# Fused convolution and gated feed-forward: the opening's mask, first convolution and the place of w_out's second half

## The chip, the cores and the metric

The kernel runs on one core of one Trainium2 chip. The metric is the device time of one execution in microseconds (us). A core has five engines with queues of their own: TensorE (PE in the profile, its weight loads PEld), VectorE (DVE), ScalarE (ACT), GpSimd (POOL) and SyncE (SP). Transfers are asked for from a queue (SPq, POOLq, ACTq) and then run in the core's DMA rings.

## The reference

Eight heads share a causal convolution of 7 taps along the sequence, its taps normalized by softmax; the result goes through a feed-forward with the gate h * cos(h).

```python
w = softmax(weight, axis=-1)                       # (8 heads, 7 taps)
out[b, s, h, :] = sum_k w[h, k] * x_pad[b, s + k, h, :]   # x: (8, 4096, 192), 24 columns a head
t = out.reshape(32768, 192)
h = t @ w_in                                       # w_in: (192, 2048)
result = (h * cos(h)) @ w_out                      # w_out: (2048, 192), float32
```

## The kernel before, in words

**Units and tiles.** The 32768 tokens are worked in 32 units of 1024 tokens (u) and 64 tiles of 512 (t); a block is 128 tokens. For each unit x is loaded in float32 (`load_unit`, L75; the rows at block edges by `load_edges`, L69), cast to bfloat16 on GpSimd (`cast_unit`, L185), convolved on TensorE by a banded matrix that holds the taps (`conv_part`, L196), evicted from PSUM (L209, L211), doubled (`double_unit`, L260) and transposed by a DMA (`turn_unit`, L269); the edges are mended on GpSimd (`mend_edges`, L288 to L300). Each tile then runs eight first matmuls h0 to h7 (`mm1`, L398; 12 or 6 matmuls of 512 columns), cosine on ScalarE and the product on VectorE (`gcu`, L405, L409), and the second matmul in 64 steps (`mm2_step`, L442), evicted and stored (L453, L456).

**Order.** Nothing is reordered by a scheduler: the program's order is the order on each engine (`manual_schedule`). `PE_ORDER`/`PE_FIRST` and `ACT_ORDER`/`ACT_FIRST` write out by hand, for each tile, the order on TensorE (h0.. first matmuls, m5 five steps of the second, c1, c2, d1, d2, r convolutions, p and q the ends of the second matmul's halves) and on ScalarE. At half of the second matmul two matmuls that share a bank are ordered by `Turn`: a no-operation in SyncE's queue (L169) waits for the one, and the other waits for it. So TensorE can stand still for whatever is ahead of that instruction in SyncE's queue, and DMAs are issued from the same queue, in order.

**Opening.** Before the loop the following is prepared:

- Four blocks of unit 0 are loaded first (SyncE, L75). GpSimd makes `quarter` (L112 to L115), then asks for w_in in two loads of 384 KB (L85), which it casts to bfloat16 on the way.
- `keep_warm` (L108) runs matmuls on zeros. One small matmul (L124) spreads the taps over partitions; softmax follows on VectorE and ScalarE (L147 to L158).
- `shifted` (L131, L132) is a diagonal of ones, 134 wide; its last 128 columns are the identity for transposes. Four copies of 32x44 of it (`rows32`, L142, L153), read with overlapping rows by the hand-made access pattern `mask`, times the taps give `prod` (L308), whose sum is `diag` (L311). When that is done SyncE goes on to the other loads of units 0 and 1. Sixteen copies spread `diag` to the banded matrix `band` (L322), on VectorE, GpSimd and ScalarE.
- `conv_first` (L340) convolves unit 0's first four blocks in four PSUM banks, quarter of the heads by quarter; four evictions (L346). After the last, SyncE loads w_out in four loads of 384 KB (L96): `load_wo(0)` the first half, `load_wo(1)` the second.
- `turn_first` (L361, L364) transposes these blocks on TensorE, since the first matmuls need them soon.
- Unit 0's other four blocks go through `conv_rest` in tile 0 (r, L196, evicted at L209) and a DMA transpose (L269), which is followed in SyncE's queue by the loads of units 2 and 3 (L75, L69) and, in tile 1, by the transpose of unit 1.
- w_out is cast on GpSimd in two halves (`cast_wo`, L92): the first in tile 0, the second after `double_unit(1)`.

Of the kernel before, what the change touches and what calls it, by code (L numbers as in the profile page):

```python
# [8 lines left out]
FP32 = mybir.dt.float32  # L9
BF16 = mybir.dt.bfloat16  # L10
AF = mybir.ActivationFunctionType
ALU = mybir.AluOpType
# [4 lines left out]
def kernel(  # L17
# [8 lines left out]
    nc = tc.nc  # L26
# [57 lines left out]
    def load_w(t):  # L84
        nc.gpsimd.dma_start(out=w[64 * t : 64 * t + 64].rearrange("p k j f -> p k (j f)"), in_=w_src[t])  # L85
# [8 lines left out]
    def load_wo(q):  # L94
        for i in range(2):
            nc.sync.dma_start(out=wo_f[:, q * HP : (q + 1) * HP, i], in_=wo_src[:, q * HP : (q + 1) * HP, i])  # L96
# [9 lines left out]
    def keep_warm(n, bank=idle):  # L106
        for _ in range(n):
            nc.tensor.matmul(out=bank, lhsT=zero[:, 0:128], rhs=zero, start=True, stop=True)  # L108
# [5 lines left out]
                            channel_multiplier=-32)  # L114
    nc.gpsimd.affine_select(out=quarter, in_=quarter, compare_op=ALU.is_ge, fill=0.0, base=31, pattern=[[-1, 128]],  # L115
                            channel_multiplier=32)
    for t in range(2):
        load_w(t)
    scrap = consts.tile([128, 1], FP32)
    nc.scalar.activation(out=scrap, in_=one, func=AF.Exp)  # L120
    keep_warm(3)
# [5 lines left out]

    xb0 = xbf_pool.tile([128, UB + 1, D], BF16, name="x_bf")

    shifted = consts.tile([128, 128 + K - 1], BF16)  # L130
    nc.gpsimd.memset(shifted, 0.0)  # L131
    nc.gpsimd.affine_select(out=shifted, in_=shifted, compare_op=ALU.not_equal, fill=1.0, base=1 - K,  # L132
                            pattern=[[1, 128 + K - 1]], channel_multiplier=-1)
    ident = shifted[:, K - 1 :]
    band = consts.tile([128, H, 256], BF16)
    nc.vector.memset(band, 0.0)

    E = 32 + K - 1
    rows32 = consts.tile([128, E + K - 1], BF16)
    mask = bass.AP(rows32.tensor, rows32.offset, [rows32.ap[0], [0, HQ], [1, E], [1, K]])  # L140
    for q in (1, 2):
        nc.gpsimd.tensor_copy(out=rows32[32 * q : 32 * q + 32], in_=shifted[0:32, 0 : E + K - 1])  # L142
    nc.gpsimd.memset(xb0[:, 0, :], 0.0)
    wn = consts.tile([128, HQ, K], BF16)

    wmax = consts.tile([128, HQ, 1], FP32)
# [2 lines left out]
    nc.vector.tensor_tensor(out=wexp, in0=w_bc, in1=wmax.to_broadcast([128, HQ, K]), op=ALU.subtract)  # L149
    nc.scalar.activation(out=wexp, in_=wexp, func=AF.Exp)  # L150
    nc.scalar.activation(out=scrap, in_=one, func=AF.Sin)
    for q in (0, 3):
        nc.vector.tensor_copy(out=rows32[32 * q : 32 * q + 32], in_=shifted[0:32, 0 : E + K - 1])  # L153
    wsum = consts.tile([128, HQ, 1], FP32)
    nc.vector.tensor_reduce(out=wsum[:, :, 0], in_=wexp, axis=mybir.AxisListType.X, op=ALU.add)
    winv = consts.tile([128, HQ, 1], FP32)
# [56 lines left out]
    def ring_banks():  # L213
        h = h_pool.tile([128, 2, T], FP32, name="h")
        return [h[:, 0, :], h[:, 1, :]]

    def o_banks():
        return [o_pools[b].tile([128, T], FP32, name="o_ps%d" % b) for b in range(2)]
# [46 lines left out]
    def turn_unit(u, n0=0, n1=UB + 1):  # L265
        ct = ct_tiles.pop(u)
        if u not in cT:
            cT[u] = cT_pool.tile([128, UB + 1, NC, 128], BF16, name="cT")
        nc.sync.dma_start_transpose(out=cT[u][:, n0:n1].rearrange("p n c k -> p (n c) k"),  # L269
                                    in_=ct[:, n0:n1].rearrange("p n c t k -> p (n c t k)"))  # L270
        cT.pop(u - 2, None)
# [13 lines left out]
    def mend_edges(u):  # L285
# [12 lines left out]
        for j in (1, 2):  # L298
# [6 lines left out]
    cast_unit(0, 0, NB, nc.scalar.copy)  # L305

    prod = consts.tile([128, HQ, E, K], BF16)
    nc.vector.tensor_tensor(out=prod, in0=mask,  # L308
                            in1=wn.rearrange("p h (o k) -> p h o k", o=1).to_broadcast([128, HQ, E, K]), op=ALU.mult)
    diag = consts.tile([128, HQ, E], FP32)  # L310
    summed = nc.vector.tensor_reduce(out=diag, in_=prod, axis=mybir.AxisListType.X, op=ALU.add)  # L311
# [20 lines left out]

    def conv_first():

        banks = o_banks() + ring_banks()
        for q in range(4):
            for n in range(NB):
                for h in range(HQ * q, HQ * (q + 1)):
                    for prev in range(2):
                        nc.tensor.matmul(  # L340
                            out=banks[n][:, 0:D].rearrange("p (k h r) -> p h k r", k=NC, h=H)[:, h],
                            lhsT=band[:, h, 128 * prev : 128 * prev + 128],
                            rhs=bf[0][:, n + 1 - prev, h * G : (h + 1) * G].rearrange("p (k r) -> p k r", k=NC),
                            start=(h == 0 and prev == 0), stop=(h == H - 1 and prev == 1), skip_group_check=True)
        for n in range(NB):
            m = copies[n % 2](out=ct_tiles[0][:, n],  # L346
                              in_=banks[n][:, 0:D].rearrange("p (m t w) -> p m t w", t=1, w=64).to_broadcast([128, NC, 2, 64]))
        tc.add_manual_dep(nc.sync.nop().ins, m.ins.name, sync_dep, reason="order of the transfers")
        load_wo(0)
        load_wo(1)  # L350

    def turn_first(half):
        banks = o_banks() if half else None
        for n in range(2):
            ps = banks[n] if half else ring_banks()
            if not half:
                if n == 0:
                    keep_warm(1, ps[1])
                ps = ps[0]
            for k in range(NC):  # L360
                nc.tensor.matmul(out=ps[:, k * 128 : (k + 1) * 128],  # L361
                                 lhsT=ct_tiles[0][:, 2 * half + n, k, :, :].rearrange("p t w -> p (t w)"), rhs=ident,
                                 start=True, stop=True, skip_group_check=True)
            copies[n](out=cT[0][:, 2 * half + n].rearrange("p c k -> p (c k)"), in_=ps[:, 0 : NC * 128])  # L364
# [118 lines left out]
    for t in range(NT + 2):  # L483
        u, second = divmod(t, TPU)
        cu, cc = (u + TPU, second) if t >= TPU else (1 + t, 1)
        conv = {"c": conv_part(cu, cc, ring_banks if t else o_banks, t < TPU) if cu < NU else iter(())}
        if t < TPU:
            conv["d"] = conv_part(cu, 0, ring_banks if t else o_banks, True)
        if t == 0:
            conv["r"] = conv_rest()  # L490
        act, done, h = (ACT_ORDER if t >= len(ACT_FIRST) else ACT_FIRST[t]).split(), set(), {}

        def flush():
            while act:
                k = act[0]
                need = {"P": "p", "Q": "p", "e": "r" if k == "er" else k[1:2] + "2"}.get(k[0], "h" + k[1:])
                if need not in done:
                    return
                act.pop(0)
                if k[0] in "PQ":  # L500
                    if 0 <= t - 2 < NT - 1:
                        evac(t - 2, "PQ".index(k[0]))
                elif k[0] == "e":
                    next(conv[k[1]], None)
                    if k == "er":
                        turn_unit(0, NB, UB)
                        load_unit(2)
                        load_edges(2)
                        cast_wo(0)
                elif k[0] == "s" and t < NT:  # L510
                    gcu(t, int(k[1]), h.pop(k[1:]), *HALVES[k[2:]])

        for k in (PE_ORDER if t >= len(PE_FIRST) else PE_FIRST[t]).split():
            if k[0] == "h" and t < NT:
                h[k[1:]] = mm1(t, int(k[1]), *HALVES[k[2:]])
            elif k[0] in conv:
                next(conv[k[0]], None)
            elif k[0] == "m":
                for q in range(step, step + int(k[1:])):
                    mm2_step(q)  # L520
                step += int(k[1:])
            elif k[0] == "p":
                assert step % (2 * STEPS) == 0
            elif k[0] == "q":
                assert step % (2 * STEPS) == STEPS
            done.add(k)
            flush()

            if k == "q":
                if second == 0 and t and u + 1 < NU:  # L530
                    mend_edges(u + 1)
                if t == 1:
                    cast_unit(3)
                    mend_edges(1)
                if second == 0 and u + 3 < NU:
                    cast_unit(u + 3)
            if k == "p":
                if second == 1 and t > 1 and cu < NU:
                    double_unit(cu)
                if second == 0 and t and u + 1 < NU:  # L540
                    turn_unit(u + 1)
                if t == 1:
                    turn_unit(1)
                if 0 <= t - 2 < NT - 1:
                    store(t - 2)
                if t == NT + 1:
                    finish(NT - 1)
            if k == ("p" if t > 1 else "q") and second == 1 and u + 4 < NU:
                load_unit(u + 4)
                load_edges(u + 4)  # L550
        if t == 0:
            double_unit(1)
            cast_wo(1)
            load_unit(3)
            load_edges(3)
            cast_unit(2)
        if t == 1:
            double_unit(2)
# [30 lines left out]
```

## Time and profile before

| what | value |
|---|---|
| median of the six times | 716.02 us (715.66 to 717.24) |
| the profiled execution, its own time | 716.02 us |
| its span, first to last instruction | 714.2 us |
| TensorE's mean granted clock | 0.997 |
| busy: PE / DVE / ACT / POOL | 703.4 / 646.5 / 589.0 / 300.0 us |
| DMA, 85.27 MB | mean 119 GB/s |
| DMA, 10 to 15 us / 15 to 20 us | 289 / 270 GB/s |

A line of the timeline reads: start, duration (both in us from the span's start), engine, source line, operation, what it writes and reads with partitions x elements, how many instructions are merged (x); in brackets the idle time of the engine before it and what ended that. A row of the windows view gives a stretch, its length, the busy time of each engine with the number of instructions in brackets (PE, PEld, DVE, ACT, POOL), TensorE's granted clock as a share of the full one, the mean busy share of the DMA engines, and GB/s. The chain of waits follows back from the last instruction to what released each step.

### The profile page before, as it was taken

The page shows a single profiled execution, that of the slowest core. Times are in us where ns is not written, and L with a number is a line of the kernel's source. Part 1 is how long each engine was busy: PE and PEld are TensorE (multiplying, and loading weights), DVE is VectorE, ACT ScalarE, POOL GpSimd, SP SyncE. Part 2 cuts the span into 40 slices and gives each one's busy share as a digit, 9 for nine tenths or more (in the row PEclk, how much of TensorE's full clock was granted, in tenths as well). Part 3 has the DMA queues.
Part 4 walks back from the last instruction along what each step waited for, and adds up shares of the span by engine and source line. Part 5 has one row for each costly group of instructions (what it writes and reads, how often), then busy time and mean ns, then how long its engine had stood idle before and what let it go on. Part 6 is the DMA issues. An engine that isn't in the chain of part 4 may idle for free.

```text
span 714.2 us, 26580 instructions
## 1 busy us (share of the span) xinstructions
PE 703.4 (98%) x11858; PEld 538.6 (75%) x11859; DVE 646.5 (91%) x603; ACT 589.0 (82%) x718; POOL 300.0 (42%) x307
## 2 busy tenths in 40 slices
PE   8899999999999999999999999999999999999997
PEld 4577777777777777777777777777777777777776
DVE  6899999999999999999999999999999999999995
ACT  5888888888888888888888888888888888888774
POOL 5563235553335542355542355523455533353200
PEclk9999999999999999999999999999999999999999
DMA  9954653545643645544536644445535456523402
GB/s 201 235 117 115 145 128 99 139 94 125 146 117 103 141 88 136 145 108 112 130 89 146 141 93 131 116 104 145 136 99 130 101 120 146 112 64 90 95 24 69
DMA packets 183714, 85.27 MB, mean 119 GB/s; under 512 B 111664, under 2 KB 183216, under 8 KB 183600
## 3 DMA queue, kind: packets, MB, share of 16 engines
q1 hardware_dynamic: 182888, 82.59, 48.7%
q8 instruction: 93, 1.52, 0.9%
q0 software_dynamic: 416, 0.79, 0.8%
q10 hardware_dynamic: 296, 0.20, 0.1%
q14 instruction: 21, 0.17, 0.1%
HBM read 31.36 MB, written 25.17 MB: 79 GB/s over the span
## 4 chain that ended last, share of the span: by engine, by line
PE 95%; DMA 1%; ACT 1%; POOL 1%; DVE 0%; issue 0%; SPq 0%; POOLq 0%
PE o_ps L442 47%; PE h L398 46%; PE h L196 3%; DMA w<-in_moe_w_in_dram 1%; ACT cs L405 1%; DVE g L409 0%; PE h L442 0%; POOL x_bf L185 0%; SPq L269 0%; ACT ct L211 0%; PE o_ps L196 0%; ACT ct L209 0%; DVE o_sb L463 0%; POOL quarter L113 0%; POOL quarter L115 0%
## 5 line engine op out<-in xcount | busy, mean ns | idle before, releaser
L409 DVE TENSOR_TENSOR g<-h,cs 128x1024 bf16<-128x1024 f32 (+1 forms) x513 | 606.0, 1220 | 32.5 <-ACT cs L405 22.1
L405 ACT ACTIVATE cs<-h 128x1024 bf16<-128x1024 f32 (+1 forms) x513 | 511.6, 1026 | 102.2 <-PE h L398 68.4
L442 PEld LDWEIGHTS <-g 64*128 64x128 bf16 x8192 | 369.2, 94 | 91.4 <-SPq L169 1.2
L442 PE MATMUL o_ps<-wo,g 64*128 64x192 bf16 x8128 | 434.6, 243 | 0.8 <-SPq L169 0.8
L398 PE MATMUL h<-cT,w 64*128 64x512 bf16 (+1 forms) x3078 | 414.0, 377 | 4.1 <-DVE g L409 2.6
L398 PEld LDWEIGHTS <-w 64*128 64x128 bf16 x3078 | 161.4, 94 | 72.2 <-issue 5.8
L294 POOL TENSOR_TENSOR edge_prod<-cT,tap 128x1008 f32<-128x1008 bf16 x30 | 67.1, 2238 | 346.6 <-DMA cT<-ct 346.6
L185 POOL CAST x_bf<-x_f 128x1728 bf16<-128x1728 f32 (+2 forms) x33 | 80.6, 2443 | 5.4 <-DMA x_f<-in_x_dram 5.2
L211 ACT CAST ct<-h 128x384 bf16<-128x384 f32 x120 | 51.7, 482 | 8.9 <-PE h L196 5.2
L453 DVE COPY o_sb<-o_ps 128x384 f32<-128x384 f32 x63 | 35.1, 557 | 23.7 <-PE o_ps L442 23.3
L260 POOL COPY ct<-ct 128x1536 bf16<-128x1536 bf16 (+1 forms) x31 | 45.7, 1473 | 4.6 <-ACT ct L211 4.6
L196 PE MATMUL h<-x_bf,band 64*128 64x192 bf16 (+1 forms) x472 | 41.0, 243 | 0.0
L299 POOL TENSOR_TENSOR edge_prod<-edge_prod 128x144 f32<-128x144 f32 x60 | 33.3, 556 | 4.7
L297 POOL TENSOR_TENSOR edge_prod<-edge_prod 128x432 f32<-128x432 f32 x30 | 30.3, 1009 | 2.4
L453 ACT COPY o_sb<-o_ps 128x384 f32<-128x384 f32 x63 | 29.9, 474 | 1.6 <-PE o_ps L442 1.6
L196 PEld LDWEIGHTS <-band 64*128 64x128 bf16 (+1 forms) x496 | 24.7, 94 | 2.2 <-issue 1.8
L300 POOL TENSOR_TENSOR cT<-edge_prod 128x144 bf16<-128x144 f32 x30 | 18.3, 608 | 2.4
L262 POOL COPY ct<-x_bf 128x192 bf16<-128x192 bf16 x60 | 19.1, 349 | 0.0
L108 PE MATMUL o_ps<-zero 128*128 128x512 bf16 x12 | 5.0, 581 | 1.3 <-DVE zero L103 1.3
L108 PEld LDWEIGHTS <-zero 128*128 128x128 bf16 x13 | 1.5, 130 | 3.5 <-issue 2.2
L463 DVE COPY o_sb<-h 128x192 f32<-128x192 f32 x1 | 0.4, 357 | 3.7 <-PE h L442 3.7
L463 ACT COPY o_sb<-h 128x192 f32<-128x192 f32 x1 | 0.3, 318 | 3.8 <-PE h L442 3.8
(63 smaller groups left out, 43.2 us busy)
## 6 DMA issues: line engine op xcount, KB each, us to landing
out_dram<-o_sb SPq DMA_DIRECT2D x63, 384.0 KB
x_f<-in_x_dram SPq DMA_DIRECT2D x30, 768.0 KB
x_f<-in_x_dram SPq DMA_DIRECT2D x31, 96.0 KB
x_f<-in_x_dram SPq DMA_DIRECT2D x4, 384.0 KB
wo_f<-in_moe_w_out_dram SPq DMA_DIRECT2D x4, 384.0 KB
w<-in_moe_w_in_dram POOLq DMA_DIRECT2D x2, 384.0 KB, 8.6
cT<-ct SPq DMA_TRANSPOSE x32
out_dram<-o_sb ACTq DMA_DIRECT2D x2, 96.0 KB
```

Of the source, the lines that this page charges most:

```text
L185: copy(out=bf[u][:, n0 + o : n1 + o, :].rearrange("p n (h k r) -> p (n h) k r", k=NC, r=R), in_=x_tiles[u][:, n0:n1, :].rearrange("p n (h ...
L196: return nc.tensor.matmul(out=ps[i // 2][:, 0 : (n1 - n0) * 2 * G].rearrange("p (n k i r) -> p i n k r", n=n1 - n0, k=NC, i=2)[:, i % 2], ...
L211: copy(o[:, :, 0, :], i[:, :, 0, :])
L260: nc.gpsimd.tensor_copy(out=ct[:, 0:nb, :, 1, :], in_=ct[:, 0:nb, :, 0, :])
L294: nc.gpsimd.tensor_tensor(out=edge_prod, in0=window, in1=tap.rearrange("p (a b k) -> p a b k", a=1, b=1).to_broadcast([128, NC * UB, K - 1 ...
L297: nc.gpsimd.tensor_tensor(out=edge_prod[:, :, :, 0:3], in0=edge_prod[:, :, :, 0:3], in1=edge_prod[:, :, :, 3:6], op=ALU.add)
L299: nc.gpsimd.tensor_tensor(out=edge_prod[:, :, :, 0], in0=edge_prod[:, :, :, 0], in1=edge_prod[:, :, :, j], op=ALU.add)
L398: nc.tensor.matmul(out=h[:, i, n0 * 128 : n1 * 128], lhsT=w[rows, k, j, :], rhs=c[rows, m0 + n0 : m0 + n1, k, :], start=(k == 0), stop=(k ...
L405: nc.scalar.activation(out=cs[:, :, part], in_=h[:, :, part], func=AF.Sin, bias=math.pi / 2.0, scale=1.0)
L409: nc.vector.tensor_tensor(out=g_tiles[t][:, 2 * j : 2 * j + 2, part], in0=h[:, :, part], in1=cs[:, :, part], op=ALU.mult)
L442: ms.append(nc.tensor.matmul(out=o_ps[tt, b, si], lhsT=g_tiles[tt][rows, f, s * 128 : (s + 1) * 128], rhs=wo[rows, f // 2, f % 2, :], star ...
L453: copies[b](o_sb[t][:, 2 * b : 2 * b + 2, :].rearrange("p s d -> p (s d)"), o_ps.pop((t, b)))
```

## The change

Six edits, all ahead of the steady loop:

1. The mask is made whole: a tile of 266 columns, set and selected by GpSimd on 32 partitions, copied to the other three groups of 32 by VectorE (one) and ScalarE (two); the four small copies go.
2. w_in is asked for behind that memset and select in GpSimd's queue.
3. The identity is a tile of its own, with a memset and a select.
4. `conv_first` works in two banks, two blocks in each, by 32 matmuls of 48 columns in place of 64 of 24, half by half, with two evictions of twice the size.
5. `turn_first` takes its banks from the ring for three of its four blocks, and runs two warm-up matmuls ahead of the first half and one ahead of the second, in place of one.
6. `load_wo(1)` is issued behind the transpose of unit 0's second half (and ahead of unit 2's load).

```diff
-    for t in range(2):
-        load_w(t)
     scrap = consts.tile([128, 1], FP32)
...
-    shifted = consts.tile([128, 128 + K - 1], BF16)
-    nc.gpsimd.memset(shifted, 0.0)
-    nc.gpsimd.affine_select(out=shifted, in_=shifted, compare_op=ALU.not_equal, fill=1.0, base=1 - K,
-                            pattern=[[1, 128 + K - 1]], channel_multiplier=-1)
-    ident = shifted[:, K - 1 :]
+    E = 32 + K - 1
+    mask = consts.tile([128, E, K], BF16)
+    nc.gpsimd.memset(mask[0:32], 0.0)
+    nc.gpsimd.affine_select(out=mask[0:32], in_=mask[0:32], compare_op=ALU.not_equal, fill=1.0, base=1 - K,
+                            pattern=[[1, E], [1, K]], channel_multiplier=-1)
     band = consts.tile([128, H, 256], BF16)
     nc.vector.memset(band, 0.0)
-
-    E = 32 + K - 1
-    rows32 = consts.tile([128, E + K - 1], BF16)
-    mask = bass.AP(rows32.tensor, rows32.offset, [rows32.ap[0], [0, HQ], [1, E], [1, K]])
-    for q in (1, 2):
-        nc.gpsimd.tensor_copy(out=rows32[32 * q : 32 * q + 32], in_=shifted[0:32, 0 : E + K - 1])
+    for q, copy in enumerate((nc.vector.tensor_copy, nc.scalar.copy, nc.scalar.copy)):
+        copy(out=mask[32 * q + 32 : 32 * q + 64], in_=mask[0:32])
+    for t in range(2):
+        load_w(t)
     nc.gpsimd.memset(xb0[:, 0, :], 0.0)
+    ident = consts.tile([128, 128], BF16)
+    nc.gpsimd.memset(ident, 0.0)
+    nc.gpsimd.affine_select(out=ident, in_=ident, compare_op=ALU.not_equal, fill=1.0, base=0, pattern=[[1, 128]],
+                            channel_multiplier=-1)
...
-    for q in (0, 3):
-        nc.vector.tensor_copy(out=rows32[32 * q : 32 * q + 32], in_=shifted[0:32, 0 : E + K - 1])
...
-    nc.vector.tensor_tensor(out=prod, in0=mask,
+    nc.vector.tensor_tensor(out=prod, in0=mask.rearrange("p (o e) k -> p o e k", o=1).to_broadcast([128, HQ, E, K]),
...
-        banks = o_banks() + ring_banks()
-        for q in range(4):
-            for n in range(NB):
-                for h in range(HQ * q, HQ * (q + 1)):
-                    for prev in range(2):
...
+        banks = o_banks()
+        for half in range(2):
+            for h in range(H):
+                for prev in range(2):
...
+            m = copies[half](out=ct_tiles[0][:, 2 * half : 2 * half + 2].rearrange("p n k t w -> p (n k) t w"),
+                             in_=banks[half][:, 0 : 2 * D].rearrange("p (m t w) -> p m t w", t=1, w=64).to_broadcast(
+                                 [128, 2 * NC, 2, 64]))
         load_wo(0)
-        load_wo(1)
...
     def turn_first(half):
-        banks = o_banks() if half else None
         for n in range(2):
-            ps = banks[n] if half else ring_banks()
-            if not half:
-                if n == 0:
-                    keep_warm(1, ps[1])
-                ps = ps[0]
+            last = half and n
+            ps = [o_pools[0].tile([128, T], FP32, name="o_ps0")] if last else ring_banks()
+            if n == 0:
+                keep_warm(2 - half, ps[1])
+            ps = ps[0]
...
                     if k == "er":
                         turn_unit(0, NB, UB)
+                        load_wo(1)
                         load_unit(2)
```

More of the change, by code (lines that the diff above doesn't have):

```diff
@@ L333, in conv_first @@
     def conv_first():
-        banks = o_banks() + ring_banks()
-        for q in range(4):
-            for n in range(NB):
-                for h in range(HQ * q, HQ * (q + 1)):
-                    for prev in range(2):
[L340 to L344, printed above, removed]
@@ L345, in conv_first @@
-        for n in range(NB):
-            m = copies[n % 2](out=ct_tiles[0][:, n],
-                              in_=banks[n][:, 0:D].rearrange("p (m t w) -> p m t w", t=1, w=64).to_broadcast([128, NC, 2, 64]))
+        banks = o_banks()
+        for half in range(2):
+            for h in range(H):
+                for prev in range(2):
+                    nc.tensor.matmul(
+                        out=banks[half][:, 0 : 2 * D].rearrange("p (n k h r) -> p h n k r", n=2, k=NC, h=H)[:, h],
+                        lhsT=band[:, h, 128 * prev : 128 * prev + 128],
+                        rhs=bf[0][:, 2 * half + 1 - prev : 2 * half + 3 - prev, h * G : (h + 1) * G].rearrange(
+                            "p n (k r) -> p n k r", k=NC),
+                        start=(h == 0 and prev == 0), stop=(h == H - 1 and prev == 1), skip_group_check=True)
+            m = copies[half](out=ct_tiles[0][:, 2 * half : 2 * half + 2].rearrange("p n k t w -> p (n k) t w"),
+                             in_=banks[half][:, 0 : 2 * D].rearrange("p (m t w) -> p m t w", t=1, w=64).to_broadcast(
+                                 [128, 2 * NC, 2, 64]))
```

## The prediction

> **What bounds the kernel now.** I began with the page: one profiled execution of 716.02 us, span 714.2, so 1.8 us lie around the span; the median of the six times shown is also 716.02, so a shift in this span is added to 716.02 as it stands.
>
> ```profile
> PE 703.4 (98%) x11858; PEld 538.6 (75%) x11859; DVE 646.5 (91%) x603; ACT 589.0 (82%) x718; POOL 300.0 (42%) x307
> PE 95%; DMA 1%; ACT 1%; POOL 1%; DVE 0%; issue 0%; SPq 0%; POOLq 0%
> ```
>
> From about 40 us on TensorE sets the pace and the diff leaves its instructions alone there: what the opening loses is lost for good, what it gains is kept. So only 0 to 40 us need reading. The timeline there has two places where PE stands still for a transfer. First, for w_in:
>
> ```profile
> 1.68 1.43 POOL L85 DMA_DIRECT2D w<-in_moe_w_in_dram  x2
> 10.47 0.27 PE L398 MATMUL h<-cT,w 64*128 64x256 bf16 x1 [0.21 <-DVE cT L364]
> 11.97 4.59 PE L398 MATMUL h<-cT,w 64*128 64x256 bf16 x29 [1.24 <-DMA w<-in_moe_w_in_dram]
> ```
>
> The transposed activations are there at 10.47 (one matmul runs), the second half of w_in only at 11.93 by the chain of waits: 1.24 us of slack for everything before it except w_in itself. Second, at the turn of the second matmul, which waits for a semaphore instruction (L169) in SyncE's own queue:
>
> ```profile
> 31.83 0.59 PE L442 MATMUL o_ps<-wo,g 64*128 64x192 bf16 x10 [0.82 <-SPq L169]
> ```
>
> SyncE comes to it only when it has issued the transpose of unit 1. Its queue in the timeline (start, duration, line):
>
> ```profile
> 9.88 4.72 SPq L96 DMA_DIRECT2D wo_f<-in_moe_w_out_dram  x4
> 18.68 1.46 SPq L269 DMA_TRANSPOSE cT<-ct  x1
> 22.45 1.53 SPq L69 DMA_DIRECT2D x_f<-in_x_dram  x1
> 25.42 6.29 SPq L269 DMA_TRANSPOSE cT<-ct  x1
> 37.02 4.87 SPq L269 DMA_TRANSPOSE cT<-ct  x1
> ```
>
> The transpose issued at 25.42 (call it T1; T0 is the one at 18.68) keeps SyncE for 6.29 us; the 32 transposes have a median of 4.44, and the next takes 4.87. What is different at 25.42 is what stands ahead of it in the rings: the loads of units 2 and 3. Unit 3's are only in at about 29.5, by the POOL cast that waits for them:
>
> ```profile
> 29.54 2.54 POOL L185 CAST x_bf<-x_f 128x1728 bf16<-128x1728 f32 x1 [0.20 <-DMA x_f<-in_x_dram]
> 33.78 0.31 POOL L288 COPY cT<-cT 128x144 bf16<-128x144 bf16 x1 [1.70 <-DMA cT<-ct]
> ```
>
> T1's issue ends at 31.71, 2.2 us after unit 3 is in. I read this as an issue that is held while the rings are full: so are the four of 384 KB at 9.88, 1.18 us each, about what 384 KB take at 320 GB/s (1.23). The windows view says how full (last two figures: DMA share, GB/s):
>
> ```profile
> 19.00:20.00 1.00, 0.27 (x3) 0.11 (x2) 0.79 (x1) 1.00 (x3) 1.00 (x1) 1.00 0.42 132
> 22.00:23.00 1.00, 1.00 (x11) 0.41 (x8) 0.89 (x2) 1.00 (x2) 0.00 (x0) 1.00 0.62 101
> 24.00:25.00 1.00, 1.00 (x21) 0.82 (x17) 0.36 (x2) 1.00 (x2) 1.00 (x1) 1.00 1.08 361
> 26.00:27.00 1.00, 1.00 (x16) 0.69 (x17) 1.00 (x2) 0.66 (x2) 1.00 (x2) 1.00 1.10 310
> ```
>
> So PE's second stop is made by the DMA rings: whatever is put into them between T0 and the x loads moves T1, and T1 moves PE.
>
> **The change, part by part.**
>
> *w_in asked for later (POOL).* A memset and a select of 32x266 now stand ahead of L85. Rows: memset 128x134 0.23, 128x256 0.31; select 128x134 0.29, 128x64 0.27. I take 0.31 + 0.34 and two gaps of 0.05: 0.75 us (bounds 0.5, the rows of 134 columns alone, to 1.1, if the select's time went by columns). The landing moves by at least as much. w_in shares the rings with x from about 9 us (the windows give 136 GB/s at 8:9, 251 at 10:11), so the 0.75 us of it left over meet that traffic: up to 1.2. I take 0.75 and keep 0.5 to 1.2. All of it is on the path: PE already waits there.
>
> *Half clock.* The granted clock is 1.00 in 9.54:12.95 and 0.50 in 12.95:16.37; in the first PE is busy 1.71 of 3.41 us. The twelve h matmuls at 13.88 take 2.68 us there, against 1.29 later. With w_in later PE is busy even less ahead of 12.95, so I keep the half clock: no gain, no further loss. The two more warm-up matmuls of turn_first (some 0.22 us each by the 0.82 us of six h matmuls, as an upper guide) run while PE would wait for evictions or for w_in: nothing, or 0.4 us inside the 1.24 of slack.
>
> *Mask, identity, first convolution.* One 32x266 copy on DVE and two on ACT replace four of 32x44 (0.17 on DVE, 0.24 on POOL). By the ACT casts (32x76 0.27, 128x384 0.48) I put 0.4 each: ACT stands idle from 2.91 to 3.75, which hides 0.8. DVE loses the 0.35 at 3.73, which stood between the exponent and its sum: 0.13 gained at diag (6.01), nothing beyond. POOL's memset and select of the identity run before 5 us, while it waits until 6.16. prod keeps its 128x532 form: 0.47, even doubled it is slack. conv_first: 64 matmuls of 24 columns over 1.7 us become 32 of 48; half 0 now needs all the band copies (done 7.92), then two evictions of 128x768. By rows (ACT 384 0.48, 1024 1.02; DVE 384 0.56, 1024 1.22) 0.80 and 0.97, side by side. ACT ends near 9.0, DVE near 9.6; the transposed first half near 10.3, the second near 11.0, against 10.25 and 10.85. w_in comes at 12.7: cost nothing, and it would take 1.7 us more to count. Different banks: each is free again before 11.
>
> *The moved load (SyncE and the rings).* Two loads of 384 KB, 0.786 MB, at 320 GB/s (the mean of 24:28): 2.46 us. Ahead of T0 they ran in 18 to 20 us, when the rings had nothing else, since T0 waits for evictions (DVE ct L209, to 18.6). T0 now comes at 18.68 + 0.75, and may start up to 0.3 sooner after its issue, as it stands behind nothing (the transpose of 37.02 moves its first bytes at 38.1; T0's come fully at about 20.0). So 19 to 20 stays empty, and all 2.46 us are put between T0 and units 2 and 3. On SyncE itself the two issues (1.1 to 1.9 each at 9.88, when rings were full; 0.4 when not) move x's by 1 to 2.5 us, before T1, whose data (POOL L260, 25.40) also come 0.75 later: no further cost.
> Unit 3 lands at 29.54 + 2.46 + 0.75 - 0.3 = 32.45. T1's issue ends 2.2 later, 34.65; PE goes on at about 34.75 instead of 31.83: **+2.9 us**. w_in's 0.75 is inside it, for PE would be ready at 31.0 + 0.75.
> Who else is late: the cast of w_out's second half (POOL, 25.34) finds its data at about 26, as it is itself 0.75 late. The cast of unit 2 (26.78) slips to about 29.2, its convolution (30.47) to 31.8: before the turn, so covered. T1 lands 2.0 after its issue, 36.7; PE wants it at 35.49 + 2.9: covered.
>
> The Trainium skill, "DMA: Bandwidth & Descriptors", Anatomy of one DMA, gives bytes / 436e3 us for the moving part of a transfer (fitted to POOL's path). By that the two loads would be an estimated 1.8 us and the sum 0.7 lower. The rows never reach that rate here, so I stay with 320 GB/s.
>
> **Rivals.**
> 1. *T1 isn't held by the backlog.* Its 6.29 may have a cause of its own (its bytes pause, 7 GB/s in 30:31, and those of the transpose of 37.02 grow thin as well, 90 GB/s in 39:40). Then it starts near 26.2, ends by 30.6 (4.44) to 32.5 (6.29), and PE is late by w_in alone, or by unit 2's convolution at 31.8 instead of 30.47: +0.6 to +1.4, 716.6 to 717.4. For it: the transposes behind no load differ by 0.8 among themselves (4.06 to 4.87). Against: only the one with x in front takes over 4.9.
> 2. *The stop costs a half-clock window besides.* PE idles some 2.1 to 2.5 us near 32 to 34.7. A window with 50% busy was followed by 0.50; one with 70% (19.78:23.19, 2.40 of 3.41) was not; here it would be between 40 and 65%. Price: up to half of 3.41, 1.7 us, less what isn't PE's: +3.5 to +5, 719.5 to 721. The Trainium skill, "TensorE: Matmul & The Clock Gate", Why this matters for your kernels, asks for no idle gap over about 3 us; by that there would be no price here. But this trace's longest gap before the 0.50 is 1.2 us, so the row speaks against the rule.
> 3. *No change to speak of*: w_in lands hardly later because x gives way, and rival 1 holds: -0.3 to +0.5.
> 4. *Faster.* T0, freed of the load ahead of it, and the loads behind it run without the two thin stretches (132 and 101 GB/s), so unit 3 is in before 28.5 and T1 done before 30.6; with the two more warm-up matmuls lifting the window before 12.95 over the bound between 50 and 70% busy, the half clock goes too: the 0.82 wait and 1.39 (2.68 - 1.29), -1.5 to -2.2, 713.8 to 714.5. It decides if the rings gain more than the 2.46 they are given; I see no row for that.
>
> **How the numbers follow.** Forecast +2.2 to +3.5 (w_in 0.5 to 1.2, rate 361 to 295 GB/s, T1's tail 1.8 to 2.5): 0.47. Rival 2: 0.17. Rival 1: 0.25. Rival 3: 0.07. Rival 4: 0.04. A measurement of this kernel tells about 0.2%, 1.43 us, from no change. Rival 1 lies within that nearly whole (0.20 of its 0.25) and so does rival 3: same 0.27; faster 0.04; slower 0.47 + 0.17 + 0.05 = 0.69. Predicted 718.9; the range 716.9 to 720.6 takes in the forecast, most of rival 2, and rival 1 from +0.9.
>
> **What would show it.** First matmul behind w_in at 12.5 to 13.2; half clock about there; T0 issued near 19.4; unit 3's cast starting at 32 to 33; T1 issue 7.5 to 8.5 us long, ended near 34.6; PE's wait for L169 2 to 3 us instead of 0.82; from there the chain's period of 10.79 us (60.43 to 71.22) as before. Wrong if T1 keeps SyncE under 6.3 us (rival 1), if a second 0.50 stretch stands at 33 to 37 (rival 2), or if h starts before 12.2 (the POOL sum).

## The result, and the profile after

The changed kernel takes 717.24 us (median of 18 runs, 714.79 to 719.25) against 716.01 us for the kernel before beside it (39 runs, 714.61 to 717.24): ratio 1.0017, interval 1.0009 to 1.0024. The profiled execution took 717.20 us at a mean granted clock of 0.997. So the kernel became slower by about 0.2%, 1.2 us, in an interval clear of no change. The prediction had +2.9 us: 718.9, with a range from 716.9 to 720.6. That the time lies inside the range, near its lower end, is luck: it is the sum of terms of both signs, most of which the prediction did not have.

The page of after, the busy line and the shares of the chain:

```profile
PE 703.7 (98%) x11828; PEld 538.5 (75%) x11829; DVE 646.3 (90%) x601; ACT 590.2 (82%) x719; POOL 300.8 (42%) x307
PE 95%; DMA 1%; DVE 1%; ACT 1%; POOL 1%; SPq 1%; issue 0%; POOLq 0%
```

Nothing moves here: the whole difference lies in the opening. Its timeline in after, the new mask, w_in's request and the first matmul h (start, duration, engine, line, operation; in brackets the idle time before):

```profile
2.05 0.96 POOL L131 TENSOR_SCALAR_AFFINE_SELECT mask<-mask 32x266 bf16<-32x266 bf16 x1
2.98 1.43 POOL L85 DMA_DIRECT2D w<-in_moe_w_in_dram  x2
10.44 1.62 PE L394 MATMUL h<-cT,w 64*128 64x256 bf16 x18 [0.18 <-DVE cT L360]
```

The select took 0.96, so w_in is asked for 1.30 later than before (2.98 against 1.68). Yet the 18 matmuls at 10.44 wait for the transposed activations only: the second of them, which waited for w_in until 11.97 before, runs at 10.54. So w_in lands some 1.4 us sooner, not 0.75 later.

SyncE's queue in after:

```profile
9.72 1.06 SPq L96 DMA_DIRECT2D wo_f<-in_moe_w_out_dram  x2
16.60 1.54 SPq L267 DMA_TRANSPOSE cT<-ct  x1
18.20 1.48 SPq L96 DMA_DIRECT2D wo_f<-in_moe_w_out_dram  x2
22.41 3.01 SPq L69 DMA_DIRECT2D x_f<-in_x_dram  x1
25.52 6.23 SPq L267 DMA_TRANSPOSE cT<-ct  x1
```

T0 goes out at 16.60 instead of 18.68, and the moved load follows at 18.20. T1 starts at 25.52, as before (25.42), and is as long. What these 2.1 us bought and what took them back is in the timeline of after, 20 to 34 us:

```profile
20.44 0.82 PE L394 MATMUL h<-cT,w 64*128 64x512 bf16 x6 [0.17 <-DMA cT<-ct]
28.20 2.50 POOL L183 CAST x_bf<-x_f 128x1728 bf16<-128x1728 f32 x1 [3.26 <-DMA x_f<-in_x_dram]
30.75 0.49 PE L194 MATMUL h<-x_bf,band 128*128 128x192 bf16 x4 [2.86 <-POOL x_bf L183]
31.00 2.51 POOL L183 CAST x_bf<-x_f 128x1728 bf16<-128x1728 f32 x1 [0.31 <-DMA x_f<-in_x_dram]
31.86 0.98 PE L438 MATMUL o_ps<-wo,g 64*128 64x192 bf16 x10 [0.59 <-SPq L167]
```

TensorE is ahead of its old times at 20.44 (tile 1 began at 22.85 before), then stands still for 2.86 us for unit 2's convolution, whose x comes late, and for 0.59 more at the turn. It passes the turn at 31.86; before, it was 31.83. All that was gained is gone by then. The windows view shows what a stop does besides (length, busy PE, PEld, DVE, ACT, POOL, granted clock, DMA share, GB/s). Before:

```profile
9.54:12.95 3.41, 1.71 (x22) 1.14 (x21) 1.31 (x3) 1.08 (x3) 0.05 (x1) 1.00 1.09 282
12.95:16.37 3.42, 3.34 (x17) 0.97 (x13) 2.51 (x3) 2.65 (x4) 3.21 (x6) 0.50 1.11 296
```

After:

```profile
12.95:16.37 3.42, 3.24 (x38) 1.54 (x34) 3.25 (x5) 2.83 (x5) 3.35 (x6) 1.00 1.03 273
28.28:31.69 3.41, 0.52 (x6) 0.43 (x5) 2.08 (x2) 0.97 (x2) 3.10 (x2) 1.00 1.07 164
31.69:35.10 3.41, 3.24 (x29) 2.02 (x30) 0.00 (x0) 1.49 (x4) 2.13 (x2) 0.50 1.09 266
```

The half-clock stretch of 12.95 is gone; a new one follows the stop, at 31.69.

**A rule for reading the runs.** A turn below is the start of the second matmul's steps behind SyncE's no-operation. Thirteen of the 17 profiled executions (before and e2 to e15, without e9 and e10) have no half-clock stretch behind the turn, and in each the time is the turn plus 683.8 to 684.4 us. In the four with one stretch there (after, e1, e9, e10) it is the turn plus 685.3 to 685.8. So what the opening does to the time is read from these two things, and after's stretch is worth some 1.4 us. One stretch of 3.41 us at half clock lowers a run's mean clock by 0.24%, so runs with none ("whole clock", mean 0.9985 or more) can be told from the rest: of 108 runs of before beside the experiments 49 had none (median 715.5; the other 59: 716.4), of the 19 runs of after on record (one more than its median is taken over) only three (714.79, 715.35, 715.69; the other 16: median 717.5).

### The profile page after: what moved, and what is told of

Same layout as the page of the kernel before. It is cut to its first block, busy times and chain, and to the rows that moved or that the text cites. A ratio compares the mean times of both kernels' runs of the same rounds, so it can differ in the third digit from the quotient of the medians.

```text
span 715.5 us, 26519 instructions
## 1 busy us (share of the span) xinstructions
PE 703.7 (98%) x11828; PEld 538.5 (75%) x11829; DVE 646.3 (90%) x601; ACT 590.2 (82%) x719; POOL 300.8 (42%) x307
## 4 chain that ended last, share of the span: by engine, by line
PE 95%; DMA 1%; DVE 1%; ACT 1%; POOL 1%; SPq 1%; issue 0%; POOLq 0%
PE o_ps L438 47%; PE h L394 45%; PE h L194 3%; DMA x_f<-in_x_dram 1%; PE h L438 0%; ACT cs L401 0%; POOL x_bf L183 0%; DVE g L405 0%; SPq L267 0%; SPq L96 0%; DVE band L320 0%; POOL mask L131 0%; PE o_ps L337 0%; ACT mask L136 0%; ACT ct L343 0%
## 5 line engine op out<-in xcount | busy, mean ns | idle before, releaser
L209 ACT CAST ct<-h 128x384 bf16<-128x384 f32 x120 | 51.7, 482 | 11.4 <-PE h L194 5.3
L92 POOL CAST wo<-wo_f 128x1536 bf16<-128x1536 f32 x2 | 2.9, 1467 | 1.3 <-DMA wo_f<-in_moe_w_out_dram 1.3
```

The costliest lines, as they stand in the source:

```text
L209: copy(o[:, :, 0, :], i[:, :, 0, :])
```

## The experiments

The theory after the comparison: the moved load costs what its ring time costs, and the other five edits gain nearly as much. The rival: the load is hidden, and the five edits do nothing. All times are medians; ratios are to before, with their intervals.

### The moved load: alone, and taken back

In before, alone (e1):

```diff
         load_wo(0)
-        load_wo(1)
...
                         turn_unit(0, NB, UB)
+                        load_wo(1)
```

> The kernel before with one edit alone: the second half of w_out is loaded behind the transpose of unit 0's second half. Theory (the moved load costs more than the whole change does, and the other edits give part of it back): unit 2's data come some 1.5 to 2.5 us later, TensorE stands at unit 2's convolution or at the turn near 30 to 34 us, and the time is 717.5 to 718.7, so more than the 1.2 us of the whole change. Rival (the moved load alone is the 1.2 us and the other edits are neutral): 717.0 to 717.4. Second rival (the load's place costs nothing and w_in asked for later is the cost): 715.8 to 716.3.

In after, put back (e2, and the same kernel once more as e12):

```diff
         load_wo(0)
+        load_wo(1)
...
                         turn_unit(0, NB, UB)
-                        load_wo(1)
```

> The changed kernel with the load of w_out's second half put back ahead of the transpose of unit 0's second half; the five other edits stay. Theory: the others give time back, since w_in lands near 10.5 us and PE loses no half-clock stretch near 13 us: 714.3 to 715.5, below the kernel before. Rival (other edits neutral): 715.8 to 716.3. Second rival (w_in asked for later is the cost): 716.8 to 717.4.

> The changed kernel with the load of w_out's second half put back, for a second profile: as e2_load_back, unit 2's convolution at 28.5 to 29.0 us, the turn at 29.4 to 30.8 us, w_in from request to landing in 5.6 to 7 us, 713.2 to 715.6.

Before, unchanged, as a measure of what single runs tell (e11):

> The kernel before, unchanged, for a second profile. Theory (the half-clock stretch near 13 us comes and goes with the phase of the clock's windows): about half of the runs at a mean clock of 1.000 and then 714.7 to 716.0, the others under 0.999 and 716.0 to 717.2; first matmul behind w_in again at 11.4 to 12.3 us. Rival (the stretch is there in each run): all runs under 0.999.

Measured: e1 720.72 us (1.0065, 1.0051 to 1.0079); e2 713.64 (0.9975, 0.9966 to 0.9985); e12 713.65 (0.9971, 0.9961 to 0.9981); e11, before unchanged, 716.86 (1.0006, 0.9997 to 1.0016). So the load costs 4.7 us alone and 3.6 in the changed kernel (717.24 against 713.64; 3.0 by the two ratios), and the five other edits gain 2.4 without it (1.8 to 2.1 by the ratios of e2 and e12). The load costs more, and the other edits gain more, than any theory or rival written before these runs had. The timeline of e2:

```profile
16.76 2.78 SPq L267 DMA_TRANSPOSE cT<-ct  x1
...
22.06 0.82 PE L395 MATMUL h<-cT,w 64*128 64x512 bf16 x6 [1.63 <-DMA cT<-ct]
25.51 2.55 POOL L183 CAST x_bf<-x_f 128x1728 bf16<-128x1728 f32 x1 [1.19 <-DMA x_f<-in_x_dram]
28.69 0.50 PE L194 MATMUL h<-x_bf,band 128*128 128x192 bf16 x4
28.80 2.55 POOL L183 CAST x_bf<-x_f 128x1728 bf16<-128x1728 f32 x1 [0.73 <-PE o_ps L439]
29.61 0.59 PE L439 MATMUL o_ps<-wo,g 64*128 64x192 bf16 x10 [0.38 <-SPq L167]
```

With the load ahead of it T0 is slower, and tile 1 starts 1.6 later than in after (22.06 against 20.44). But the casts of units 2 and 3 can start 2.69 and 2.20 sooner than in after (28.20, 31.00), the convolution at 28.69 waits for nothing, and the turn is at 29.61, 2.25 sooner. What T0 gains by going out early is lost again: the x loads decide when TensorE goes on. In e1's timeline the same is seen, bigger:

```profile
31.16 2.51 POOL L185 CAST x_bf<-x_f 128x1728 bf16<-128x1728 f32 x1 [3.00 <-DMA x_f<-in_x_dram]
33.72 0.49 PE L196 MATMUL h<-x_bf,band 128*128 128x192 bf16 x4 [1.85 <-POOL x_bf L185]
34.74 0.59 PE L441 MATMUL o_ps<-wo,g 64*128 64x192 bf16 x10 [0.49 <-SPq L169]
```

and its windows show half clock twice, once by w_in's wait (two stretches in a row) and once behind the stop:

```profile
11.43:18.26 6.83, 5.98 (x39) 3.79 (x40) 3.42 (x4) 3.24 (x4) 4.64 (x6) 0.50 0.92 254
...
31.89:35.30 3.41, 1.08 (x18) 0.97 (x20) 2.35 (x2) 1.91 (x5) 3.21 (x2) 1.00 1.06 179
35.30:38.70 3.40, 3.40 (x32) 2.06 (x28) 1.12 (x1) 1.49 (x3) 1.40 (x2) 0.50 1.03 289
```

e11's profiled execution (before, unchanged) is a warning on single records: the cast of unit 3 at 30.89 instead of 29.54 and the turn at 33.21 instead of 31.83. The verdicts therefore rest on medians, the profiles only tell where.

### Half of the moved load

After, with the first 384 KB ahead of T0 and the second behind it (e5):

```diff
-    def load_wo(q):
-        for i in range(2):
+    def load_wo(q, parts=(0, 1)):
+        for i in parts:
...
         load_wo(0)
+        load_wo(1, (0,))
...
-                        load_wo(1)
+                        load_wo(1, (1,))
```

> The changed kernel with one of the two DMAs of w_out's second half put back ahead of the transpose of unit 0's second half, so 384 KB are moved and not 768. Theory (the ring time put between that transpose and unit 2's data is the price): unit 2's convolution comes 1.2 us sooner than the 30.75 us of the changed kernel, the transpose still lands near 20.4 us because the rings have some 1.2 us free ahead of it, and the time is 713.6 to 715.2. Rival (any load behind the transpose costs the same, by its issue or its place in the queue): 716.5 to 717.5.

Measured: 714.05 us (0.9985, 0.9971 to 0.9998); at whole clock 713.67 (7 of 12 runs), as e2's 713.53. In its profile the cast of unit 3 starts at 29.14 and the turn is at 29.99. So in the runs at whole clock half the load behind T0 costs nearly nothing. But the other five runs stand at 716.4 to 717.2, where the slower five of e2 and e12 stand at 715.1 to 715.7, so the mean is 715.0 against 714.1. Half the load costs about 1 us on average and the whole 3.0 to 3.6: the cost is not in proportion to the bytes.

### The stop and the half clock

After, with twelve matmuls on zeros ahead of unit 2's convolution, where TensorE stands (e6); they add nothing to the result:

```diff
+            if u == 2 and c == 0:
+                keep_warm(12, ps[1])
```

> The changed kernel with twelve matmuls on zeros (about 2.6 us) where TensorE stands for unit 2's data, ahead of unit 2's convolution; they add no result. Theory (half clock behind this stop is a part of the price): no stretch of granted clock 0.50 near 31 to 35 us, fewer runs at a mean clock under 0.999, median 715.3 to 716.3, so 1 to 2 us under the changed kernel. Rival (the stop itself is the whole price): 716.9 to 717.6.

Measured: 715.94 us (0.9997, 0.9988 to 1.0006), and all 11 runs at whole clock. The windows of e6, as of after above:

```profile
28.28:31.69 3.41, 2.90 (x18) 1.40 (x15) 2.16 (x2) 0.79 (x2) 3.00 (x2) 1.00 0.87 125
31.70:35.10 3.40, 3.02 (x46) 2.00 (x48) 0.69 (x1) 2.56 (x6) 2.36 (x2) 1.00 1.08 259
```

TensorE is busy 2.90 of 3.41 us where it was 0.52, and the next stretch stays at 1.00. The turn is no sooner (32.08), yet the kernel is 1.3 us faster than after (1.4 by the ratios): this is the price of the half clock behind the stop, shown by itself. The Trainium skill ("TensorE: Matmul & The Clock Gate", Why this matters for your kernels) asks that no idle gap between bursts of matmuls exceed about 3 us. By it after's gaps of 2.86 and 0.59 would do no harm; here a window with them, and e1's with gaps of 1.85 and 0.49, was followed by 0.50. The measurement decides: a longest gap of about 3 us is no safe bound.

The busy share of the window orders the rows better, but it doesn't settle them either. The windows can be counted in steps of 3.41 us from a change of the clock, at the end of the profile if there is none in the opening. So counted, e3 (below) has a full clock behind a window with 1.62 us busy and a gap of 1.79, and e1 half clock behind one with 1.94 busy; first e3, then e1:

```profile
19.41:22.82 3.41, 1.62 (x20) 0.78 (x18) 2.66 (x3) 2.51 (x4) 2.27 (x3) 1.00 0.80 212
22.82:26.23 3.41, 3.41 (x58) 2.34 (x56) 2.68 (x4) 3.18 (x4) 2.07 (x2) 1.00 1.05 310
```

```profile
8.02:11.43 3.41, 1.94 (x36) 1.30 (x33) 2.11 (x4) 1.72 (x4) 0.00 (x0) 1.00 1.05 177
```

In the 17 profiles, from 5 us to 45 us, a full-clock window with 1.5 us busy or less was always followed by 0.50 and one with 2.0 or more never; from 1.6 to 1.97 both occur. What the clock goes by there isn't shown.

e5 with four such matmuls at the same place (e10):

> The changed kernel with half of the moved load put back (as e5_half_load) and four matmuls on zeros ahead of unit 2's convolution, where TensorE then stands some 0.9 us. Theory (the slower runs of e5_half_load, 716.4 to 717.2, are those with a half-clock stretch): hardly any run under a mean clock of 0.999, median 713.4 to 714.2, no run over 715.5. Rival (the slower runs have another cause): a part of the runs stays at 716 to 717.

Measured: 714.49 us (0.9981, 0.9970 to 0.9993), no better than e5. Ten of 12 runs were at whole clock, but they spread from 713.13 to 715.63, so the clock isn't all that varies between runs. In the profiled one T1 took 7.95 us and TensorE waited 1.92 at the turn, ahead of a half-clock stretch at 32.2; T1 may be what varies in the others too, which their times alone don't show.

### Where the five edits gain

Only w_in's request moved, in before (e3: behind the copies of `shifted`, asked at 2.72, as in the diff; e9: the same two lines just behind its select, at 2.20; against 1.68):

```diff
-    for t in range(2):
-        load_w(t)
...
+    for t in range(2):
+        load_w(t)
     nc.gpsimd.memset(xb0[:, 0, :], 0.0)
```

> The kernel before with w_in asked for behind the diagonal of ones and two of its copies (about 1.2 us later in GpSimd's queue), nothing else. Theory of the prediction, that the landing moves with the request: first matmul behind w_in at 13 us, 716.5 to 717.0. Rival (w_in in the kernel before was slowed by x loads still in the rings, and takes about 6 us from a later request): first matmul at 10.5 to 11.5 us, 714.8 to 716.0.

> The kernel before with w_in asked for behind the memset and select of the diagonal of ones only, about 0.65 us later than before and 0.6 us sooner than in e3_w_late_alone. Theory (w_in is slowed only where its first packets meet the first x load, which is in by about 4.3 us): request to landing of the two loads 5.6 to 7 us as in the late requests, first matmul free of w_in at 10.5 us, 714.2 to 715.0. Rival (the later the request the shorter the transfer, by something that runs on): 6.5 to 8.5 us to landing, first matmul near 11 us, 714.8 to 715.8.

Measured: e3 714.65 us (0.9985, 0.9976 to 0.9993), e9 714.45 (0.9981, 0.9973 to 0.9990). Asking later alone is worth 1.1 to 1.4 us by the ratios, 1.4 to 1.7 by the medians of before beside them. The view of the tile w ends with the time from request to landing of its two loads; before, then e3:

```profile
DMA to landing us min/median/max: 7.8/8.6/9.4
```

```profile
DMA to landing us min/median/max: 5.7/6.2/6.8
```

and e3's first matmuls h no longer wait for w_in:

```profile
10.46 1.59 PE L398 MATMUL h<-cT,w 64*128 64x256 bf16 x18 [0.21 <-DVE cT L364]
```

The loads are over 2 us shorter when asked 1.04 us later; e9's lie between (6.5/7.3/8.2). The Trainium skill ("DMA: Bandwidth & Descriptors", Rules for kernel authors) advises issuing a DMA early and waiting for it late. For w_in the measurement went the other way.

A reading of it: the early request meets the first x load, which is in at about 4.3 us, and loses by that. To test it, x was put behind w_in instead, in before (e7: SyncE's first x load waits for `band`'s memset, by a dependency of its own):

```diff
-    load_unit(0, 0, NB)
...
-    nc.vector.memset(band, 0.0)
+    cleared = nc.vector.memset(band, 0.0)
...
+    load_unit(0, 0, NB)
```

> The kernel before with the first four blocks of x asked for about 1.5 us later (behind VectorE's clearing of the band), w_in asked for as before. Theory (w_in is slowed where its start overlaps x in the rings): they now overlap wholly, w_in's first matmul comes at 12.0 to 13.0 us, time 716.0 to 717.5. Rival (w_in is slow for another reason, such as an early request): first matmul near 11.5 to 12.0 us as before, 715.8 to 716.5.

Measured: 718.28 us (1.0035, 1.0023 to 1.0047). It tests little: x itself came late, the cast of unit 0 waited 4.57 us for it, and the first matmul h was at 14.99. Only its first load of w_in speaks for the reading: it took 5.8 us, the second 8.9. A graded dependence on the request's time fits e9 as well. The cause stays open.

The convolution and transposes of after, in before: both (e4), both without the added warm-up matmuls (e8, `keep_warm(1 - half, ps[1])`), `conv_first` alone (e14), `turn_first` alone (e15). The edits are those of the change; their core, first of `conv_first`, then of `turn_first`:

```diff
-        banks = o_banks() + ring_banks()
-        for q in range(4):
-            for n in range(NB):
...
+        banks = o_banks()
+        for half in range(2):
+            for h in range(H):
...
-        banks = o_banks() if half else None
...
+            if n == 0:
+                keep_warm(2 - half, ps[1])
```

> The kernel before with only the first convolution in two banks and the transposes on TensorE with their banks and warm-up matmuls as in the changed kernel. Theory: all of it lies inside the wait for w_in, 715.8 to 716.3, first matmul of the first stage still released by w_in near 11.9 us. Rival (the warm-up matmuls keep the clock whole past 13 us): no half-clock stretch near 13 us, 714.6 to 715.5.

> The kernel before with the first convolution in two banks and the new banks of the transposes on TensorE, but with one warm-up matmul ahead of the first half and none ahead of the second (as before in number). Theory (the added warm-up matmuls keep the clock whole past 13 us and that is the gain of 2 us): half of the runs at a mean clock under 0.999 again, 715.3 to 716.2. Rival (the gain is in the convolution and its evictions): 713.8 to 714.5.

> The kernel before with the first convolution in two banks alone; the transposes on TensorE keep their banks and their one warm-up matmul. Theory (the gain of e4 and e8 is in the convolution): 713.6 to 714.5, all runs at a whole clock, first matmul behind w_in near 11.5 us. Rival (it is in the transposes' banks): 715.7 to 716.5.

> The kernel before with only the new banks and warm-up matmuls of the transposes on TensorE; the first convolution stays in four banks. Theory (the gain of e4 and e8 is in the convolution): 715.5 to 716.5. Rival (it is in the transposes' banks): 713.6 to 714.5.

Measured: e4 713.99 us (0.9972, 0.9962 to 0.9982), e8 713.69 (0.9969, 0.9957 to 0.9981), e14 714.02 (0.9977, 0.9968 to 0.9985), e15 716.10 (0.9998, 0.9989 to 1.0007). So the two-bank convolution with its two evictions gains 1.7 us by itself (e14 against 715.77, the median of before beside it), and the banks and warm-ups of `turn_first` nothing that can be told from noise. In e14 TensorE still waits for w_in, timeline:

```profile
11.86 1.47 PE L398 MATMUL h<-cT,w 64*128 64x256 bf16 x17 [1.12 <-DMA w<-in_moe_w_in_dram]
```

nearly as long as before (1.24, to 11.97), and yet no half clock follows, and its turn is at 29.68. One reason in this record is where the wait falls: it lies across two windows, 7.58:10.99 and 10.99:14.40, with TensorE busy 2.53 and 2.11 us, where before's lies whole in one with 1.71. But it can hardly be chance alone: of the 24 runs of e4, e8 and e14, 22 were at whole clock. Is that the whole gain? In before, six matmuls on zeros fill the wait for w_in (e13):

```diff
     turn_first(1)
+    keep_warm(6, ring_banks()[1])
```

> The kernel before with six matmuls on zeros behind the transposes on TensorE, where it stands for w_in; they add no result. Theory (what the convolution edit brings is a clock that stays whole past 13 us): hardly a run under a mean clock of 0.9985, and then the median of the kernel before's own whole-clock runs or a little less, 715.2 to 715.7. Rival (the whole 2 us come with the clock): 713.8 to 714.5. Second rival (the clock's loss there has another cause than the stop): half of the runs still under 0.9985, 715.8 to 716.5.

Measured: 715.39 us (0.9994, 0.9985 to 1.0003), all 11 runs at whole clock. So a whole clock alone brings about 0.4 us, in an interval that includes no change, or 0.9 by the two medians of the 108 runs of before. The two-bank convolution brings more than that. In the records it goes along with a w_in that is in sooner for the same request (11.4 to 11.9 against 11.9 to 12.7 with four banks) and, mostly, a T1 that ends sooner behind unit 3 (below). A part of w_in's lead is there before the convolution runs at all: from 5.00 to 6.80 us the rings move 146 to 163 GB/s in e4, e8 and e14 and 104 to 125 in before, e1, e11, e13 and e15, all with w_in asked for at 1.68. So the order and size of the convolution's own matmuls can't be the whole reason; what is stays open.

The gains don't add: by the medians beside them w_in late brings 1.4, two banks 1.7, both with the rest 2.4. The fastest kernels are e2 (713.64), e8 (713.69) and e4 (713.99): they beat both kernels, and no combination tried went below.

## Why the prediction was right or wrong

The turn is where the prediction made its sum, and it can be taken apart in the records of before, e2 (five edits) and after: the cast of unit 3 starts at 29.54, 28.80 and 31.00; T1's issue ends 2.17, 0.70 and 0.75 after it. These are single records, and others of the same kernels differ: the cast of unit 3 starts at 30.89 in e11 (before again) and at 29.18 in e12 (e2 again).

| term | predicted | measured |
|---|---|---|
| unit 3, by w_in and the other edits (before to e2) | +0.75 | -0.74 |
| unit 3, by the moved load (e2 to after) | +2.46 - 0.3 | +2.20 |
| T1's end behind unit 3 | 2.2, unchanged | 0.75: -1.42 |
| the turn | +2.9 | +0.04 |
| half clock behind the stop | none | about 1.3 |

- **The moved load, right.** Ring time at 320 GB/s, less 0.3 for the earlier T0, is 2.16; the records have 2.20 from e2 and 1.82 from e12. That it falls between T0 and the x loads, and that the x loads set when TensorE goes on, is shown by e2. The median's cost is more, 3.6; the half clock, some 1.3, comes on top.
- **Failed step: "The landing moves by at least as much. ... All of it is on the path."** The request moved by more than forecast (1.30, the select taking 0.96 for its 0.34), and the landing moved the other way, by some 1.4 us. e3 shows that asking later is enough for that.
- **Failed step: the first convolution, "cost nothing".** It gains 1.7 us (e14). The prediction looked for what the edits cost and where cover hides it, never for what they release: w_in's wait was taken as independent of everything ahead of it, and the half clock as kept.
- **Mis-sized term: T1's tail, "2.2 later".** It is not a constant of the ring backlog. The profiled executions have two values, 0.70 to 0.84 or 1.84 to 2.23: the short one in seven of nine records with the two-bank convolution, the long one in seven of eight with the old one. So T1 stayed at 6.23 us in spite of the load ahead of it. What the two differ by is a pause of 1.0 to 1.5 us in T1's bytes, seen in the DMA packets (by the windows view 7 GB/s from 30.17 to 31.17 in before, 5 GB/s from 30.44 to 31.44 in e2). The tail is long where the pause lies between the last bytes of unit 3 and the end of T1's issue, as in before (issue ended at 31.71). It is short where the pause falls under the end of the x loads (after, e1, e6) or comes when the issue has ended (e2, where it ended at 29.50, e4, e5, e12, e14). What sets the moment of the pause is open.
- **Failed step: "before the turn, so covered".** Unit 2's cast was put at 29.2 and its convolution at 31.8, hidden behind a turn at 34.75. They came at 28.20 and 30.75, and as the turn came much sooner, the convolution became the main stop: 2.86 us of it against 0.59 at the turn.
- **Half clock.** "Kept" at 13 us was wrong: PE busy 2.79 of 3.41 there instead of 1.71. But rival 2's stretch behind the stop came true, as its rows said (e6: 1.3 us).
- **The rivals.** Rival 1 has the number (716.6 to 717.4) by another way: T1 is moved by the x loads, and w_in alone is a gain. Rival 4's price fits the five edits without the load (-1.5 to -2.2 foreseen, -2.4 measured by e2), though not its causes, a T0 freed of the load and the warm-up matmuls (e15: nothing). The gain came together with the load's cost, while the prediction had treated the two as excluding each other.

## What to carry to other kernels

A load that is moved behind a small urgent transfer is not hidden if a bigger urgent one stands behind it in the rings: price it by its ring time against the next transfer that an engine waits for, and ask whether the small one was late at all. A wait for a DMA is not a constant: later requests and other neighbours may shorten it, so bound it on both sides. Price a stop of the matrix engine with the half-clock stretch that may follow it (here some 1.4 us), and read from the windows whether it came: neither the longest gap nor the busy share told it in every case.

## What was not expected of the hardware

- Two loads of 384 KB from GpSimd's queue, cast on the way, took 7.6 to 10.2 us when asked for at 1.68 us with the old convolution, 6.7 to 9.3 with the two-bank one (e4, e8, e14), and 5.6 to 6.9 when asked for at 2.7 to 3.0 (after, e2, e3).
- The granted clock fell to 0.50 behind windows with TensorE busy 0.52, 1.08, 1.71 and 1.94 of 3.41 us, with no gap over 2.86, and stayed whole behind one with 1.62. The windows' bounds differ between executions of one kernel (12.95 in before's record, 12.07 in e11's), and 49 of 108 runs of before kept a whole clock.
- The bytes of one DMA transpose paused for 1.0 to 1.5 us (5 to 7 GB/s in before and e2), and where that pause fell moved the end of its issue by 1.4 us.
- A select over 32x266 with a pattern of two dimensions took 0.96 us, one of 128x134 0.29 and of 128x128 0.50.
